# Two x loads on two queues ahead of the activation table load, and a landing reserve in the planner of a fused attention and GLU kernel

## The chip, the cores and the metric

The kernel runs on one core of one Trainium2 chip. The metric is the device time of one execution in microseconds; a smaller number is better. Executions of this kernel carry a span (first to last instruction) and the mean clock granted to TensorE; the time is the span plus about 2 us. Medians and lists of executions take in all of a run. The runs below were made on different chips; kernels ran with the kernel before beside them, and are compared with that.

Names used below: TensorE does matmuls (PE in the profile), VectorE is DVE, ScalarE is ACT, SyncE is SP. In the kernel before, all loads but two and all stores are issued by SyncE. A clock of 1.00 is full speed.

## The reference, cut to what matters

```python
xn = layernorm(x)                          # x: 1 x 2048 x 512, bf16
out = x + A(xn) + B(xn)
# A: linear attention, 32 heads of 16, feature map = softmax(+q W_phi), softmax(-q W_phi)
# B: h = (xn @ w_gate) * (xn @ w_up)       # 512 -> 1792
#    h @ w_down                            # 1792 -> 512
```

Everything waits for normalised tokens. There are 16 tiles of 128 tokens. Tiles 0 to 3 are loaded first, tiles 4 to 7 by one load of 512 KB, called x4 below.

## The kernel before: the parts that matter

Every instruction is a "step" with an estimated cost. A list scheduler in the Python file fixes the order of each engine from these estimates; the program gives each engine its instructions in that order, with waits on semaphores between engines. So an estimate that is wrong does no harm to the results, but it can put an instruction that must wait in front of one that need not. For loads:

```python
# in _plan(): when does a load land?
d0 = max(start + st.cost + 1500.0, dma_free)
dma_free = d0 + st.nbytes / 305.0          # ns, one queue of 305 GB/s
st.finish = dma_free
```

The issue order of the loads at the start:

```python
sc.step(ACT, ... preload_act_table_set("natural_log_exp_and_others"), name="tbl")
sc.step(ACT, ... activation(out=dum, in_=one1, func=Exp), name="dum")
load_x(SP, 0, 1)                # x0: tile 0, 128 KB
load_x(SP, 1, 1)                # x1: tile 1
load_gu(SP, "g", 0, 2)          # wg0: first gate slice
load_gu(ACT, "u", 0, 2)         # wu0: first up slice
# ... cut: further slices, in the order of the chain ...
sc.chain("x0 x1 wg0 x2 wg2 wu2 wg4 wu4 wT1 wv x4 wg8 wu8 x8 x12")
sc.chain("tbl dum wu0")
```

A unit U of the GLU takes two PSUM banks of a ring of six. ScalarE frees the gate bank, VectorE frees the up bank by the multiply:

```python
def U(ft, sg):
    bg, bu = nb(), nb()                                    # ring of six banks
    mm(group(bank(bg), ...wg...)); act_op(g, bank(bg))     # ScalarE frees bg
    mm(group(bank(bu), ...wu...))
    dve(... h = bank(bu) * g ..., name=f"h{ft}.{sg}")      # VectorE frees bu
```

The layer norm of a tile is, on VectorE, statistics (`bn_stats`, names st4, st5, ...), an aggregate (ag4), and, after two small ScalarE steps, the scaling. At the point that matters TensorE runs U(4), U(5), then a small product called FOLD, whose fourth part takes the bank that h4.0 (the multiply of U(4)) frees.

The softmax here doesn't subtract the row's maximum and nothing guards it: scores larger than these inputs give would overflow.

## Time and profile before

| quantity | value | view |
|---|---|---|
| median of the timed executions | 225.05 us (224.85 to 225.13) | times |
| time of the execution that was profiled | 227.54 us, span 225.5, clock 0.992 | times |
| TensorE busy | 218.3 us, 97% of the span | busy table |
| VectorE busy | 152.4 us, 68% | busy table |
| largest hole of TensorE | 1.96 us at 19.75 us | timeline |
| clock granted, 20 to 25 us | 0.69 on average | windows |

The timeline of TensorE of the kernel before. Columns: start in us, duration, engine, line, operation, output and input, shape, count, and in brackets the idle time before it and what ended it:

```profile
5.86 0.40 PE L448 MATMUL ps<-arena 128*128 128x128 bf16 x4 [0.73 <-DVE arena L576]
6.61 2.29 PE L448 MATMUL ps<-arena 128*128 128x128 bf16 x36 [0.35 <-DVE arena L576]
9.07 2.37 PE L448 MATMUL ps<-arena 128*128 128x256 bf16 x24 [0.17 <-DMA arena<-in_B_w_up_dram]
11.96 7.79 PE L448 MATMUL ps<-arena 128*128 128x256 bf16 x60 [0.53 <-ACT arena L420]
21.71 201.21 PE L448 MATMUL ps<-arena 128*128 128x128 bf16 x1174 [1.96 <-DVE arena L709]
```

The holes are in the brackets. The line at 11.96 is the narrow units and the first two wide ones, 7.79 us without a hole. Then TensorE waits 1.96 us for line 709, the multiply.

The timeline of VectorE of the same kernel shows why the multiply came late:

```profile
16.08 0.42 DVE L720 TENSOR_TENSOR arena<-ps,arena 128x256 bf16<-128x256 f32 x1 [0.45 <-ACT arena L420]
19.77 1.29 DVE L568 BATCH_NORM_STATS2 arena<-arena 128x6 f32<-128x512 bf16 x2 [3.27 <-DMA arena<-in_A_x_dram]
20.98 0.67 DVE L709 TENSOR_TENSOR arena<-ps,arena 128x512 bf16<-128x512 f32 x1
21.57 0.24 DVE L570 BATCH_NORM_AGGREGATE arena<-arena 128x2 f32<-128x6 f32 x2
```

VectorE was idle for 3.27 us until x4 landed, then did two statistics (1.29 us), and only then the multiply at 20.98, although U(4) was done at about 18.3 us (an estimate: in the changed kernel, below, the multiply starts as soon as TensorE has delivered, 6.30 us after the wide stage begins at 11.38; here that stage begins at 11.96). The chain of waits says the same; columns are start, duration and what it was:

```profile
12.34 7.41 DMA arena<-in_A_x_dram
...
20.39 0.68 DVE arena L568
21.06 0.60 DVE arena L709
...
21.71 200.79 PE ps L448 x1170
```

The windows view (stretch, its length, busy time and count of PE, weight loads, DVE, ACT, POOL, granted clock, DMA share, GB/s) shows what followed the hole:

```profile
20.00:25.00 5.00, 3.29 (x12) 1.37 (x13) 3.82 (x10) 3.13 (x9) 0.00 (x0) 0.69 0.82 268
25.00:30.00 5.00, 5.00 (x24) 2.25 (x23) 4.37 (x10) 2.25 (x5) 0.00 (x0) 0.97 0.28 58
```

For about 3.3 us TensorE ran at half clock (finer windows show 0.50 from about 21.95 to 25.3 us). Last, the end of the kernel, VectorE's last two instructions and SyncE's last two stores:

```profile
222.52 0.86 DVE L810 TENSOR_TENSOR arena<-ps,arena 128x256 bf16<-128x256 f32 x2 [2.56 <-PE ps L448]
222.97 0.81 SPq L172 DMA_DIRECT2D out_dram<-arena  x2
```

From VectorE's last instruction (222.52 + 0.86 = 223.38) to the end of the span (225.5) it is 2.12 us.

### The profile page before, as it was taken

The numbers are of one execution on the slowest core, as the hardware profiler recorded it, in microseconds if no ns is written. First come the engines' busy times: TensorE is split into PE (matmuls) and PEld (weight loads), VectorE is DVE, ScalarE is ACT, GpSimd is POOL, SyncE is SP. The second block draws the span as 40 slices with busy tenths as digits, with TensorE's granted clock in tenths as the row PEclk, the third lists the DMA queues.
The fourth block names the chain that finished last, engine by engine and source line by source line (L and its number), as shares of the span: only waits on it lengthen the run. The fifth ranks groups of instructions, "written<-read, shape, count | busy, mean of one in ns | idle before, by whom it ended". The sixth has DMA issues, their size and how long they took to land.

```text
span 225.5 us, 3354 instructions
## 1 busy us (share of the span) xinstructions
PE 218.3 (97%) x1308; PEld 108.3 (48%) x1308; DVE 152.4 (68%) x309; ACT 78.0 (35%) x160; POOL 38.7 (17%) x52
## 2 busy tenths in 40 slices
PE   7896999999999999999999999999999999999995
PEld 2763344444554454455444444444444444444454
DVE  3854699999958866779666548448447565745541
ACT  3642744543474334445212322222221321321100
POOL 5300011221131113122111101101101101101100
PEclk9999799999999999999999999999999999999999
DMA  6999347584300000002571334232132223124032
GB/s 178 312 270 374 92 101 127 120 274 117 49 0 0 3 0 0 1 3 47 116 79 40 93 93 26 70 93 70 26 93 70 54 67 93 30 63 96 29 88 71
DMA packets 48015, 19.89 MB, mean 88 GB/s; under 512 B 36848, under 2 KB 48000, under 8 KB 48000
## 3 DMA queue, kind: packets, MB, share of 16 engines
q1 hardware_dynamic: 47440, 19.41, 36.5%
q10 hardware_dynamic: 528, 0.26, 0.4%
q8 instruction: 10, 0.16, 0.3%
q14 instruction: 5, 0.04, 0.1%
q0 software_dynamic: 32, 0.02, 0.0%
HBM read 8.67 MB, written 2.10 MB: 48 GB/s over the span
## 4 chain that ended last, share of the span: by engine, by line
PE 89%; SPq 5%; DMA 3%; DVE 1%; issue 1%
PE ps L448 89%; DMA arena<-in_A_x_dram 3%; SPq L171 2%; SPq L172 2%; DVE arena L810 0%; DVE arena L568 0%; DVE arena L709 0%
## 5 line engine op out<-in xcount | busy, mean ns | idle before, releaser
L448 PE MATMUL ps<-arena 128*128 128x512 bf16 (+3 forms) x1298 | 214.1, 327 | 3.7 <-DVE arena L709 2.0
L448 PEld LDWEIGHTS ps<-arena 128*128 128x128 bf16 x1298 | 107.0, 98 | 111.3 <-DVE arena L709 2.4
L420 ACT ACTIVATE arena<-ps 128x512 bf16<-128x512 f32 (+2 forms) x138 | 72.6, 573 | 120.2 <-PE ps L448 120.0
L641 DVE TENSOR_REDUCE arena<-arena 128x64 f32<-128x1024 bf16 x32 | 38.8, 1213 | 39.3 <-ACT arena L420 39.3
L649 POOL TENSOR_TENSOR arena<-arena 128x512 bf16<-128x512 bf16 x32 | 33.8, 1055 | 171.2 <-DVE arena L647 171.2
L709 DVE TENSOR_TENSOR arena<-ps,arena 128x512 bf16<-128x512 f32 x52 | 35.4, 682 | 8.3 <-PE ps L448 7.6
L568 DVE BATCH_NORM_STATS2 arena<-arena 128x6 f32<-128x512 bf16 x16 | 10.4, 677 | 6.0 <-DMA arena<-in_A_x_dram 6.0
L793 DVE TENSOR_TENSOR arena<-ps,arena 128x512 bf16<-128x512 f32 x15 | 10.4, 690 | 4.1 <-PE ps L448 4.0
L768 DVE TENSOR_TENSOR arena<-ps,arena 128x512 bf16<-128x512 f32 x16 | 11.1, 691 | 0.6
L670 DVE TENSOR_TENSOR arena<-ps,arena 128x512 bf16<-128x512 f32 x16 | 10.2, 636 | 0.4 <-PE ps L448 0.4
L659 DVE RECIPROCAL arena<-arena 128x64 f32<-128x64 f32 x16 | 8.6, 538 | 0.0
L420 ACT ACTIVATE arena<-arena 128x2 f32<-128x2 f32 (+1 forms) x20 | 4.9, 252 | 10.3 <-DVE arena L570 9.9
L576 DVE TENSOR_SCALAR arena<-arena 128x512 bf16<-128x512 bf16 x16 | 6.1, 413 | 0.4 <-ACT arena L420 0.3
L647 DVE TENSOR_TENSOR arena<-arena 128x32 f32<-128x32 f32 x32 | 5.9, 184 | 0.4
L764 DVE RECIPROCAL arena<-arena 128x32 f32<-128x32 f32 x16 | 5.6, 352 | 0.5
L744 DVE RECIPROCAL arena<-arena 128x32 f32<-128x32 f32 x16 | 5.6, 351 | 0.4
L762 DVE SCALAR_TENSOR_TENSOR arena<-arena,ps 128x32 f32<-128x32 f32 x16 | 2.8, 172 | 4.2 <-PE ps L448 4.2
L819 PE MATMUL ps<-const-bfloat16-1.0 128*128 128x512 bf16 x10 | 4.3, 613 | 0.8 <-PEq L936 0.8
L673 DVE CAST arena<-arena 128x32 bf16<-128x32 f32 x16 | 4.6, 285 | 0.0
L720 DVE TENSOR_TENSOR arena<-ps,arena 128x256 bf16<-128x256 f32 x6 | 2.5, 421 | 2.3 <-ACT arena L420 2.3
L819 PEld LDWEIGHTS ps<-const-bfloat16-1.0 128*128 128x128 bf16 x10 | 1.3, 139 | 3.0 <-issue 3.0
L570 DVE BATCH_NORM_AGGREGATE arena<-arena 128x2 f32<-128x6 f32 x16 | 2.6, 166 | 0.2
(18 smaller groups left out, 11.3 us busy)
## 6 DMA issues: line engine op xcount, KB each, us to landing
out_dram<-arena SPq DMA_DIRECT2D x15, 128.0 KB, 2.0
arena<-in_B_w_down_dram SPq DMA_DIRECT2D x1, 1792.0 KB, 7.7
arena<-in_A_x_dram SPq DMA_DIRECT2D x3, 512.0 KB, 11.1
arena<-in_B_w_gate_dram SPq DMA_DIRECT2D x1, 768.0 KB, 9.0
arena<-in_B_w_up_dram SPq DMA_DIRECT2D x1, 768.0 KB, 10.5
arena<-arena SPq DMA_TRANSPOSE x44, 2.5
arena<-in_B_w_gate_dram SPq DMA_DIRECT2D x2, 256.0 KB, 5.1
arena<-in_B_w_gate_dram SPq DMA_DIRECT2D x1, 512.0 KB, 6.5
```

The source lines that it names most:

```text
L420: return e.activation(out=out_ap, in_=in_ap, func=func, scale=scale, **kw)
L448: ins = e.matmul(o, lhsT=l, rhs=r, start=s, stop=p, skip_group_check=True)
L568: dve(lambda e, t=t: e.bn_stats(stats_v[:, t, :], x_tile(t)), [x_tile(t)], [stats_v[:, t, :]], cost=560.0, name=f"st{t}", win=win)
L576: dve(lambda e, t=t: e.tensor_scalar(out=xn_tile(t), in0=x_tile(t), scalar1=mv_v[:, t, 0:1], scalar2=rstd_v[:, t:t + 1], op0=ALU.subtract, ...
L641: dve(lambda e: e.tensor_reduce(out=sm, in_=Et.rearrange("p (h f) -> p h f", f=16), axis=AX.X, op=ALU.add), [Et], [sm], cost=1130.0, name= ...
L647: dve(lambda e: e.tensor_tensor(out=ratio, in0=smv[:, :, 0], in1=rc, op=ALU.mult), [sm, rc], [ratio], cost=100.0, name=f"{name}q{t}")
L649: pool(lambda e: e.tensor_tensor(out=ev[:, :, 1, :], in0=ev[:, :, 1, :], in1=ratio[:, :, None].to_broadcast([128, H, 16]), op=ALU.mult), [ ...
L659: dve(lambda e: e.reciprocal(out=rs, in_=sm), [sm], [rs], cost=500.0, name=f"kc{t}")
L670: dve(lambda e: e.tensor_tensor(out=o1, in0=src, in1=rp_[:, :, :, None].to_broadcast([128, 8, 4, 16]), op=ALU.mult), [src, rs_v[:, t % 4, ...
L709: dve(lambda e: e.tensor_tensor(out=h, in0=bank(bu), in1=g, op=ALU.mult), [bank(bu), g], [h], name=f"h{ft}.{sg}")
L768: dve(lambda e: e.tensor_tensor(out=ov, in0=src, in1=wv4[:, :, :, None].to_broadcast([128, 8, 4, 16]), op=ALU.mult), [src, w], [o], cost=6 ...
L793: dve(lambda e: e.tensor_tensor(out=o, in0=bank(b), in1=x_tile(t), op=ALU.add), [bank(b), x_tile(t)], [o], name=f"fin{t}")
```

## The change

Its intent: x1 no longer queues behind x0 on SyncE, all later SyncE loads go out one slot sooner, and the planner stops believing in early landings, so that no engine has a waiting instruction ahead of one that is ready.

```diff
-                st.finish = dma_free
+                st.finish = dma_free + (2500.0 if st.nbytes > 300000 else 0.0)
...
-    alloc("dum", 32)
...
-    sc.step(ACT, lambda e: e.preload_act_table_set("natural_log_exp_and_others"), cost=1300.0, lat=0.0, name="tbl")
-    dum = sbv("dum", 0, 1)
-    one1 = nc.const_aps.tensor(1.0, [128, 1], BF16)
-    sc.step(ACT, lambda e: e.activation(out=dum, in_=one1, func=ACTF.Exp), writes=[dum], cost=120.0, name="dum")
     load_x(SP, 0, 1)
-    load_x(SP, 1, 1)
+    load_x(ACT, 1, 1)
     load_gu(SP, "g", 0, 2)
     load_gu(ACT, "u", 0, 2)
+    sc.step(ACT, lambda e: e.preload_act_table_set("natural_log_exp_and_others"), cost=1300.0, lat=0.0, name="tbl")
...
-    sc.chain("x0 x1 wg0 x2 wg2 wu2 wg4 wu4 wT1 wv x4 wg8 wu8 x8 x12")
-    sc.chain("tbl dum wu0")
+    sc.chain("x0 wg0 x2 wg2 wu2 wg4 wu4 wT1 wv x4 wg8 wu8 x8 x12")
+    sc.chain("x1 wu0 tbl")
```

The first line is the largest edit, since every order on TensorE, VectorE and ScalarE is planned anew from it.

## The prediction

> **What bounds it.** TensorE is the chain: 89% of the span in the chain of waits, busy 218.3 of 225.5 us (busy table). The timeline of TensorE shows 3.7 us of holes after the warm-up matmuls, all before 21.7 us: 0.73 (waits for the first normalised tile), 0.35 (the second), 0.17 (second up slice, a DMA), 0.53 (ScalarE copying a transpose), 1.96 at 19.75. After 21.71 us it runs 201 us without a recorded wait.
>
> **The large hole.** The wait list says TensorE waits 2.0 us for one VectorE multiply (gate times up, which frees a PSUM bank). That multiply was not short of data: the VectorE timeline is empty from 16.50 to 19.77, held by a DMA: the statistics of x tile 4, whose 512 KB load lands at 19.75. VectorE runs in order, two statistics (1.29 us) were planned ahead of the multiply, because the planner in the kernel thought x4 would land some 3 us sooner. TensorE then pays twice: the windows view grants clock 0.50 from about 21.96 to 25.3 us; weight loads of 512-wide matmuls are 0.427 us apart there, 0.213 elsewhere, so about 1.7 us is lost. The Trainium skill ("TensorE: Matmul & The Clock Gate", Part 1) describes this half clock after idleness; the trace agrees (427 ns against about 213). The hole's price is therefore 1.96 + 1.7 = 3.7 us.
>
> **What the change does.** (a) Loads over 300 KB count as landing 2.5 us later in the plan. All engine orders are planned from that, so the multiplies of the first wide units (bank releases) should go ahead of x4's statistics. Same work, other order. (b) x1 moves to ScalarE's queue, ahead of its first up slice; the table load (1.28 us) follows, and a dummy activation (0.20 us) goes. SyncE issues one load less at the start: 0.47 us sooner for all later ones. The table load should run about 1.8 to 3.1 us, before ScalarE's first work at 4.29, so it stays hidden.
>
> **How much is critical.** (a) nearly all of 3.7 us, if no hole of that size comes back. Give-back, estimated 0.3: x4's loads still land at about 19.4; a multiply that is ready then may sit behind a statistics instruction (0.68). VectorE is 90% or more busy from 28 to 62 us, and TensorE will be 3.7 us further ahead, with the six banks as its slack. (b) x1's statistics waited 0.34 us for the DMA; that goes. But the second up slice lands at 9.06 us and TensorE already waited 0.17 for it; the skill ("DMA: Bandwidth & Descriptors", Issuing engines are not separate DMA queues) says that queues share the 16 engines, and the windows show them saturated from 3 us (about 300 GB/s), so the bytes ahead of that slice stay and it lands at most slightly sooner. I estimate 0.15 us of gain.
>
> Sum: 225.05 - 3.7 + 0.3 - 0.15 = 221.5 us (1.6% faster). Range 220.2 to 223.9. Chances: faster by over 2% 0.2, within 2% 0.77, slower 0.03.
>
> **What would show it.** The 1.96 us hole gone from the TensorE timeline; clock 1.0 in the windows from 20 to 26 us; on VectorE the multiply of the first wide unit before the first statistics of x4; x1's statistics with no DMA wait; first real matmul at about 5.5 instead of 5.86; the wait for the second up slice longer than 0.17. No new wait on TensorE after 22 us above 0.5 us.
>
> **What would make it wrong.** A new stall past 1.5 us[...]: at 20 to 24 us for the large gate and up loads (landing 21.9 and 23.9), or at 30 to 60 us for VectorE. Then 223 to 225. If all startup holes shrink too, 220.

## The result, and the profile after

The changed kernel took 224.06 us (median; 224.03 to 224.61, 4 executions), the kernel before 225.09 us (224.85 to 225.50, 4 executions). The ratio is 0.9958, 95% interval 0.9937 to 0.9979: 0.4% faster. Ratios here and below are the mean time of one kernel's fast runs over that of the other's of the same rounds, so they are not quite the ratio of the medians quoted. The forecast of 221.5 us, range 220.2 to 223.9, was missed.

At first sight the profile contradicts the times. Its span fell from 225.5 to 222.0 us, by 3.5 us, just as predicted. The timeline of TensorE of the changed kernel:

```profile
5.47 0.40 PE L447 MATMUL ps<-arena 128*128 128x128 bf16 x4 [0.20 <-DVE arena L572]
6.18 4.68 PE L447 MATMUL ps<-arena 128*128 128x128 bf16 x60 [0.32 <-DVE arena L572]
11.38 207.18 PE L447 MATMUL ps<-arena 128*128 128x256 bf16 x1211 [0.53 <-ACT arena L419]
```

The hole at x4 is gone, the start is 0.58 us earlier at the third line, and no wait follows. VectorE of the changed kernel:

```profile
17.68 0.69 DVE L705 TENSOR_TENSOR arena<-ps,arena 128x512 bf16<-128x512 f32 x1 [1.75 <-PE ps L447]
18.29 0.68 DVE L564 BATCH_NORM_STATS2 arena<-arena 128x6 f32<-128x512 bf16 x1
18.89 0.68 DVE L705 TENSOR_TENSOR arena<-ps,arena 128x512 bf16<-128x512 f32 x1
```

The multiply (line 705 now) runs at 17.68, as soon as TensorE has delivered, ahead of the first statistic of x4. The clock in the windows view stays full:

```profile
20.00:25.00 5.00, 4.95 (x24) 2.24 (x23) 4.72 (x13) 3.93 (x11) 0.00 (x0) 1.00 0.95 268
```

And the end of the changed kernel:

```profile
218.17 0.86 DVE L806 TENSOR_TENSOR arena<-ps,arena 128x256 bf16<-128x256 f32 x2 [2.46 <-PE ps L447]
218.62 1.11 SPq L172 DMA_DIRECT2D out_dram<-arena  x2
```

From VectorE's last instruction (219.03) to the end (222.0) it is 2.97 us, 0.85 more than before. The two last stores take 1.11 us of SyncE instead of 0.81.

The contradiction is resolved by the times of the two profiled executions themselves. The one of before took 227.54 us, 2.5 us over its own median; the one of after took 224.04 us, its median. In both the time is the span plus 2.04 us. So the profile of before was not of an ordinary execution, and 2.5 of the 3.5 us are the difference between that execution and an ordinary one. That the spans differ by just what was forecast is luck: the 3.5 us are 0.58 of an earlier wide stage, 1.96 of the hole and 1.82 of a shorter run after it (201.21 - 199.39, where 199.39 is 207.18 less the 7.79 before the place of the hole), less 0.86 of a longer end.

### The profile page after: what moved, and what is told of

The parts are those of the page before. It is cut to its first block, busy times and chain, and to the rows that moved or that the text cites. A ratio compares the mean times of both kernels' runs of the same rounds, so it can differ in the third digit from the quotient of the medians.

```text
span 222.0 us, 3327 instructions
## 1 busy us (share of the span) xinstructions
PE 215.4 (97%) x1285; PEld 107.9 (49%) x1308; DVE 152.1 (69%) x309; ACT 78.0 (35%) x159; POOL 38.8 (17%) x52
## 4 chain that ended last, share of the span: by engine, by line
PE 94%; DVE 1%; DMA 1%; ACT 1%; issue 1%
PE ps L447 94%; DMA arena<-in_A_x_dram 1%; ACT arena L419 1%; DVE arena L564 1%; DVE arena L806 0%; DVE arena L566 0%; DVE arena L572 0%
## 5 line engine op out<-in xcount | busy, mean ns | idle before, releaser
L447 PE MATMUL ps<-arena 128*128 128x512 bf16 (+3 forms) x1275 | 211.0, 325 | 2.3 <-ACT arena L419 0.5
```

Source lines behind the costliest of these rows:

```text
L447: ins = e.matmul(o, lhsT=l, rhs=r, start=s, stop=p, skip_group_check=True)
```

## The experiments

Theory A: an ordinary execution of before has a smaller hole at x4 and no half clock, so there was only about 1 us to win. Rival theory B: the 3.7 us are lost in every execution of before, and the changed kernel gives 2.7 us back. After the first four runs two more theories were needed, for the end: C, it depends on what SyncE has gone through before; D, it belongs to something else in the changed kernel.

### The kernel before again

No edit; five rounds, for the span and clock of each execution.

> The kernel before, unchanged, run again for the span and clock of each execution. Theory A (the profiled execution of before, whose own time was 227.54 us against a median of 225.05, was an unusual one with a late x4 load): spans near 223.0 us, time minus span about 2.0 us as in both profiled executions, clock 0.998 to 1.000 in nearly all, and, if the profile is of an ordinary execution, a hole of 0.3 to 1.2 us instead of 1.96 and no half clock. Theory B (the hole of 3.7 us is in every execution and the changed kernel gives 2.7 us back elsewhere): spans near 225.5 us with clock 0.992, hole 1.9 us.

Measured: 225.07 us. The six spans are 222.9 to 223.8 us, the clock 0.999 or 1.000 in five of them and 0.992 in one. The profiled execution, again the slowest of its set (225.77 us), has this on TensorE:

```profile
11.75 7.79 PE L448 MATMUL ps<-arena 128*128 128x256 bf16 x59 [0.53 <-ACT arena L420]
21.23 200.00 PE L448 MATMUL ps<-arena 128*128 128x128 bf16 x1152 [1.69 <-DVE arena L709]
```

and this in the windows view:

```profile
20.00:25.00 5.00, 3.64 (x19) 1.48 (x20) 4.22 (x11) 3.47 (x10) 0.00 (x0) 1.00 0.84 274
```

The hole is there, 1.69 us, but no half clock follows it. Spans are those of theory A; the hole is longer than it expected, but in an execution that was 0.7 us over its median. If that excess is all in the hole, an ordinary one is about 1.0 us (an estimate from these two numbers; no profile of an execution at the median was taken). Theory B falls.

This profile also prices the half clock. TensorE's run after the hole is 200.00 us here and was 201.21 us in the first profile: 1.2 us more, not the 1.7 that the forecast took from the clock alone. The timeline of the weight loads (PEld, 20 to 30 us) shows where the rest may have gone. Just after the hole they wait twice at full clock:

```profile
22.55 0.55 PEld L448 LDWEIGHTS ps<-arena 128*128 128x128 bf16 x4 [0.55 <-DVE arena L709]
23.66 6.37 PEld L448 LDWEIGHTS ps<-arena 128*128 128x128 bf16 x31 [0.56 <-ACT arena L420]
```

In the first profile no pause just after the hole was longer than 0.28 us, and these came at every weight load; the slower matmuls took up time that is waited away otherwise.

### The changed kernel again

> The changed kernel again, same chip and rounds as the others. Both theories: 224.0 us, span 222.0, clock 1.000, no hole at x4.

Measured beside it: 224.18 us, 0.9963 of before (0.9950 to 0.9976), six spans from 222.0 to 222.6, clock 0.998 or more in all, no hole at x4:

```profile
11.73 207.30 PE L447 MATMUL ps<-arena 128*128 128x256 bf16 x1211 [0.53 <-ACT arena L419]
```

Set against the profile of before of the same chip, the difference of the spans (223.8 and 222.4) splits without a rest:

| part | before | changed | gain |
|---|---|---|---|
| wide stage of TensorE starts at | 11.75 | 11.73 | 0.02 |
| hole at x4 | 1.69 | 0 | 1.69 |
| TensorE from there to its last matmul | 200.00 | 199.51 (207.30 - 7.79) | 0.49 |
| TensorE's last matmul to the end | 2.57 | 3.37 | -0.80 |
| span | 223.8 | 222.4 | 1.40 |

7.79 us is the stretch of TensorE before the hole in the kernel before, which the changed kernel runs through in one piece of 207.30 us. The 0.49 us after the hole lie mostly in the two waits of the weight loads shown above: 0.55 and 0.56 us there, and in this profile (PEld, 19 to 30 us)

```profile
20.47 0.55 PEld L447 LDWEIGHTS ps<-arena 128*128 128x128 bf16 x4 [0.36 <-DVE arena L705]
21.23 8.85 PEld L447 LDWEIGHTS ps<-arena 128*128 128x128 bf16 x42 [0.21 <-ACT arena L419]
```

which is 0.54 us less.

### The reserve alone

```diff
-                st.finish = dma_free
+                st.finish = dma_free + (2500.0 if st.nbytes > 300000 else 0.0)
```

> The reserve of 2.5 us alone; x1 stays on SyncE's queue, table load and dummy first. TensorE's order is then that of the changed kernel, SyncE's that of before. Theory A: the ordinary hole goes, worth 0.3 to 1.2 us, so 224.0 to 224.8 us, and the hole at the first tiles stays (first real matmul at about 5.86 us). Theory B: about 221.7 us if the order is the cure of 3.7 us and something else in the change gives it back; 224.5 or more if the new order itself gives it back.

Measured: 224.43 us, ratio 0.9966 (0.9940 to 0.9993), within the noise of the whole change (0.9963). TensorE:

```profile
9.53 2.37 PE L448 MATMUL ps<-arena 128*128 128x256 bf16 x24 [0.51 <-DMA arena<-in_B_w_up_dram]
12.43 207.26 PE L448 MATMUL ps<-arena 128*128 128x256 bf16 x1211 [0.53 <-ACT arena L420]
```

No hole at x4; TensorE runs 207.26 us without a wait after 12.43, so the gain of about 0.5 us after the hole comes with the new order. The end is 2.05 us, the old length. The executions spread from 223.47 to 225.16 us; in the profiled one (224.22) TensorE waits 0.51 us at 9 us for the second up slice. That the spread comes from late first loads, which the hole had hidden, would fit, but is not shown; one execution (225.16) also had a clock of 0.992.

### The queue alone

```diff
-                st.finish = dma_free + (2500.0 if st.nbytes > 300000 else 0.0)
+                st.finish = dma_free
```

against the changed kernel, so x1 and wu0 stay on ScalarE's queue.

> x1 and the first up slice on ScalarE's queue ahead of the table load, dummy gone, no reserve. TensorE's order is that of before. On VectorE three statistics of x4 now stand ahead of the first wide multiply instead of two. Theory A: first real matmul at about 5.47 us, start gain 0.4 to 0.6 us, but TensorE reaches the multiply's wait that much sooner and x4's load does not land that much sooner, so the hole grows and the time stays within 0.3 us of before, or gets worse if the hole is long enough for the half clock (then up to 226 us). Theory B: 224.5 us, the start gain kept.

Measured: 226.23 us, ratio 1.0052 (1.0035 to 1.0068). This half of the change makes the kernel slower. TensorE and VectorE:

```profile
21.13 199.83 PE L447 MATMUL ps<-arena 128*128 128x128 bf16 x1152 [1.64 <-DVE arena L705]
```

```profile
18.53 1.29 DVE L564 BATCH_NORM_STATS2 arena<-arena 128x6 f32<-128x512 bf16 x2 [2.29 <-DMA arena<-in_A_x_dram]
...
19.82 0.66 DVE L564 BATCH_NORM_STATS2 arena<-arena 128x6 f32<-128x512 bf16 x1
20.40 0.67 DVE L705 TENSOR_TENSOR arena<-ps,arena 128x512 bf16<-128x512 f32 x1
```

x4 lands sooner (18.53 against 19.30 in the profile of before of the same chip), but the planner believed in it sooner still and put a third statistic ahead of the multiply, so the hole is 1.64 us. The end is 2.78 us, the long one. Start gain: none worth the name, the wide stage starts at 11.70 against 11.75. Against an ordinary execution of before, 0.67 us of longer end (2.78 - 2.11) and about 0.6 us of longer hole (1.64 less the estimate of 1.0) add up to 1.3 us; measured is 1.20 (226.23 - 225.03). The third statistic (0.66 us) more than took back what the sooner landing gave.

### Only the landing of x4, sooner and later

Two neighbouring loads are exchanged on SyncE after planning, so that TensorE, VectorE and ScalarE keep the order of before, the statistics ahead of the multiply included.

```diff
+    # later run: ("x4", "wg8") in place of ("wv", "x4")
+    for lst in (new_order[SP], global_order):
+        i, j = [next(k for k, st in enumerate(lst) if st.name == n) for n in ("wv", "x4")]
+        lst[i], lst[j] = lst[j], lst[i]
     sc.by_eng = new_order
```

> Kernel before with only two neighbouring loads of SyncE exchanged, x4 ahead of wv, after planning, so that all other engines keep the order of before, the two statistics ahead of the first wide multiply included. x4 should land about 1.6 us sooner (512 KB at about 330 GB/s). Theory A (in an ordinary execution of before the hole is only about 1.1 us and set by x4's landing): hole gone, clock 1.000, time about 224.1 us, 1.0 below before. If the order itself, or the half clock, cost 3.7 us in ordinary executions: 221.5 us.

Measured: 223.34 us against 225.33 (ratio 0.9922, 0.9874 to 0.9970; some of the executions of before beside it ran at the half clock). Without the executions under clock 0.995 the medians are 223.28 and 225.11, 1.8 us apart. TensorE has no hole from 11.58 us on:

```profile
11.58 207.73 PE L451 MATMUL ps<-arena 128*128 128x256 bf16 x1234 [0.53 <-ACT arena L423]
```

```profile
17.39 1.29 DVE L571 BATCH_NORM_STATS2 arena<-arena 128x6 f32<-128x512 bf16 x2 [1.26 <-DMA arena<-in_A_x_dram]
18.59 0.67 DVE L712 TENSOR_TENSOR arena<-ps,arena 128x512 bf16<-128x512 f32 x1
```

x4 lands at 17.39, and the two statistics are over before TensorE needs the bank. Repeated on another chip, beside the changed kernel:

> The exchange of x4 and wv alone in the kernel before, again, now on the same chip as the changed kernel: 223.3 us as the first time, 0.8 us under the changed kernel, with a single execution at the half clock (clock 0.992) about 1.6 us longer.

Measured: 224.13 us against 225.15, ratio 0.9956 (0.9934 to 0.9977). The first value was not reproduced: here the gain is 1.0 us (1.2 without the executions under clock 0.995), not 1.8, and this kernel isn't ahead of the changed one on the same chip (223.89, below). In its profile a hole of 0.16 us is left:

```profile
19.73 199.99 PE L451 MATMUL ps<-arena 128*128 128x128 bf16 x1174 [0.16 <-DVE arena L712]
```

Both runs together say that the ordinary hole is worth 1.0 to 1.8 us, and that the arrival of x4 alone, with the old order, sets it.

> Kernel before with x4 exchanged with the load after it (768 KB), all other engines in the order of before. x4 lands about 2.4 us later, so the hole is about 3.5 us instead of 1.1. If the half clock comes only with a hole long enough, it should now come in every execution: clock 0.99 or less, and the time rises by 2.4 plus about 1.7, to 229 us. If the half clock was a chance event of one profiled execution, the time rises by 2.4 alone, to 227.4, with clock 1.000.

Measured: 229.97 us, ratio 1.0197 (1.0129 to 1.0264, wide), with executions from 227.44 to 231.09, the last of them slow. The profiled one is the fastest:

```profile
22.77 200.00 PE L451 MATMUL ps<-arena 128*128 128x128 bf16 x1174 [3.49 <-DVE arena L712]
```

A hole of 3.49 us, as expected, and clock 1.000 in this execution: 227.44 us, the value expected without half clock. The other four have clocks of 0.992, 0.993, 0.985 and 0.985 and take 0.5 to 3.7 us longer. So a lowered clock came far more often here (4 of 5 executions), but not always. In the kernel before a clock under 0.995 was seen in 6 of the 38 executions of the experiments. Four of those six (224.96, 225.04, 225.16, 225.36 us) are no longer than their neighbours, two (227.28 and 228.10, the latter slow and left out of the ratios) are 2 to 3 us longer, as the first profiled one was. Where the half clock fell in unprofiled executions can't be told, since only their spans and mean clocks are known. The hole at x4 can't be behind all of it: 4 of the 51 executions of the repeated runs whose profile has no hole there, or one of 0.16 us, had such a clock too (225.16 in the reserve alone, 224.89 and 225.13 with x4 sooner, 225.42 with the load of 16 rows below).

### The end: does SyncE's past set it?

The length of the end was 2.05 to 2.13 us in all profiles with x1 on SyncE and 2.78 to 2.97 with x1 on ScalarE's queue. SyncE's instructions were counted in the built programs: 93 before the change and 92 after it (no view of the profile shows this count). First, a useless load was added in the quiet middle of the changed kernel, of 128 rows or of 16 (the lines that reserve the scratch area are cut here and below):

```diff
+    sc.dma(SP, scratch[0:128, :], x_flat[128:256, :], 131072, writes=[scratch[0:128, :]], name="pad")   # or 16 rows
-    sc.chain("x12 ... xT14 xT15")
+    sc.chain("x12 ... xT14 xT15 pad")
```

> The changed kernel with one useless load more on SyncE's queue, in the middle of the kernel (128 rows of 1 KB, the same as the load that had left that queue, into a scratch area nobody reads), so that SyncE again issues as many loads of as many rows as before. All engine orders else are those of the changed kernel. In the traces with x1 on ScalarE's queue the last store's issue starts 0.36 us after its data is ready (0.03 without), and the span ends 2.8 to 3.0 us after VectorE's last instruction instead of 2.1. Theory C (that end depends on what SyncE's queue or instruction stream has gone through before): the end goes back to 2.1 us, time 223.4 us against 224.2. Theory D (the end is something else of the changed kernel, or the queue of ScalarE being used): unchanged, 224.2 us.

> As the run with the 128-row useless load, but only 16 rows of 1 KB: one instruction more on SyncE, but an eighth of the rows. Theory C1 (the number of SyncE's instructions sets the end): 223.4 us, end 2.1 us, as with 128 rows. Theory C2 (the number of rows that went through SyncE's queue sets it): end stays at 2.8 to 3.0 us, 224.2 us, while 128 rows give 2.1. Theory D: both unchanged.

Measured: 223.76 us (end 2.06) and 223.70 us (end 2.07). The short end is back in both, so the number of rows doesn't matter. Theory D falls. Then a SyncE instruction that is no load:

```diff
+            # cut: by_name, a table of the steps by name
+                if st.name == "wo":
+                    for q in ("x0", "wg0"):                      # landed long ago
+                        e.wait_ge(dma_sems[by_name[q].lane[1]], 16)
```

> The changed kernel with one SyncE instruction more that is no DMA (waits for loads long complete, before the load of wo), 93 SyncE instructions as before the change instead of 92, but 32 plain DMA copies as in the changed kernel and no byte more. If the number of SyncE's instructions sets the length of the end: 2.1 us from VectorE's last instruction to the end, 223.5 us. If the number of DMAs issued on SyncE sets it: 2.8 to 3.0 us, 224.2 us.

Measured: 223.46 us, ratio 0.9927 (0.9907 to 0.9946), end 2.10 us:

```profile
218.94 0.86 DVE L810 TENSOR_TENSOR arena<-ps,arena 128x256 bf16<-128x256 f32 x2 [2.46 <-PE ps L451]
219.38 0.81 SPq L172 DMA_DIRECT2D out_dram<-arena  x2
```

The two last stores take 0.81 us again. The changed kernel on the same chip:

> The changed kernel again, same chip as the three others: 224.2 us, end 2.9 us.

Measured: 223.89 us, ratio 0.9943 (0.9924 to 0.9961), end 2.92 us:

```profile
218.12 0.86 DVE L806 TENSOR_TENSOR arena<-ps,arena 128x256 bf16<-128x256 f32 x2 [2.47 <-PE ps L447]
218.57 1.11 SPq L172 DMA_DIRECT2D out_dram<-arena  x2
```

One waiting instruction that does nothing shortens the end by 0.8 us in the profiles. In the times it is 0.43 us in the medians (223.89 to 223.46), which is not clear of the noise: the means of the six and six executions differ by 0.37 us, with a 95% interval from -0.1 to 0.9. The profile of the version with the wait also has 0.53 us of waiting for an up slice at its start, which that of the changed kernel has not.

Last, other counts of SyncE instructions, one look each (91: another load moved to ScalarE's queue, which spoils the start; 94, 96, 100: more idle waits).

> Changed kernel with the last load of x on ScalarE's queue as well: 91 SyncE instructions (its start may be slower, only the end is looked at). If any count below 93 is bad: end 2.8 to 3.0 us after VectorE's last instruction. If 92 alone is bad, or a period: 2.1 us.

> Changed kernel with two SyncE instructions more that only wait for loads long complete: 94. End 2.1 us in all cases except a period of 2 (then 2.9).

> Four SyncE instructions more: 96. End 2.1 us, or 2.8 to 3.0 if the bad count recurs every 4.

> Eight SyncE instructions more: 100. End 2.1 us, or 2.8 to 3.0 if the bad count recurs every 8 (or 4).

| SyncE instructions | end in us (one per profile) | last transfer of the queue q14, us from VectorE's last instruction |
|---|---|---|
| 91 | 2.11 | 1.4 after |
| 92 (changed kernel and queue alone) | 2.97, 2.91, 2.92, 2.78 | 0.9 to 1.2 after |
| 93 | 2.12, 2.11, 2.05, 2.13, 2.07, 2.11 (x1 on SyncE); 2.06, 2.07, 2.12, 2.10 (x1 on ScalarE's queue) | 1.0 to 1.2 before |
| 94 | 2.13 | 1.7 before |
| 96 | 2.09 | 6.5 before |
| 100 | 2.12 | 16 before |

Of the counts tried only 92 has the long end, in all four profiles; 91, 94, 96 and 100 have one profile each. They speak against a period of 1, 2, 4 or 8. That one SyncE instruction more brings the short end back is shown in four versions. The cause is not shown, but the traces hold a candidate, in the last column. The DMA view lists two queues of the kind "instruction", q8 and q14. The last transfer of q14, one packet of 0.01 MB, comes earlier the more instructions SyncE has. With 93 and more it lands before the last stores are issued, with 91 when their data have been moved. With 92 it falls between the last two stores, in all four profiles. The DMA view of the changed kernel (the repeat above, 219.5 to 220.5 us in 40 slices) shows it:

```profile
GB/s 287 328 328 369 185 184 124 62 21 0 0 0 0 0 0 0 0 0 0 0 0 328 0 0 0 0 0 82 123 184 266 287 287 328 328 206 184 103 62 21
q14 instruction: 1, 0.01, 3.9%
```

The first stretch is the next-to-last store, the single slice of 328 at 220.03 is q14, and the last store moves only after it. So SyncE probably waits for its own instructions at that point. No run moved this transfer without also changing the count, so it stays an inference.

### Both

The changed kernel with the useless 16-row load and with x4 ahead of wv:

> The changed kernel with the 16-row useless load (which gave the short end back) and with x4 ahead of wv on SyncE's queue; TensorE, VectorE and ScalarE keep the order of the changed kernel. In the changed kernel VectorE waits about 0.3 us for x4 after its first wide multiply, and TensorE does not feel it. So if the gains do not add (theory: both cures remove the same hole), it runs at 223.5 us like the padded kernel; if an earlier x4 still helps with the new order, 222.9 us or less.

Measured: 223.43 us, six executions from 223.19 to 223.64, ratio 0.9922 (0.9906 to 0.9937). It equals the kernel with the idle wait (223.46), so an earlier x4 adds nothing in the median where the order is already right. On the same chip both versions beat the kernel before (225.15). Against the changed kernel (223.89) this one is faster by 0.48 us in the means, 95% interval 0.2 to 0.8; for the idle wait alone the times don't show it, as said above.

## Why the prediction was wrong, point by point

**What failed: "The hole's price is therefore 1.96 + 1.7 = 3.7 us", with "(a) nearly all of 3.7 us" as the gain.** The mechanism was right: two statistics waiting for x4 stand ahead of the multiply, and the reserve puts it in front. The size was read from one execution that wasn't ordinary. In most executions (32 of 38) the half clock, 1.7 us of the 3.7, is absent, and even where it was profiled the run after the hole was only 1.2 us longer. The ordinary hole is about 1.0 us by the estimate above and worth 1.0 to 1.8 us by the exchange of loads. So the term of 3.7 us was really 1.0 to 1.8 us. The warning was at hand: the profiled execution took 227.54 us against a median of 225.05. Its own time should have been charged first: if that excess lies in the hole and the clock, 3.7 - 2.5 = 1.2 us is left for an ordinary execution.

The Trainium skill ("TensorE: Matmul & The Clock Gate", Part 1) says that the clock follows the activity in a window of 4096 cycles, 3413 ns, that runs freely and does not start with the kernel, so that clock changes vary from run to run. The prediction cited the page but used the half clock as a fixed price. The runs agree with the page so far as the one drop seen in a profile lasted about 3.3 us, and as the same program drops in some executions and not in others. The length of the hole alone didn't decide it: 1.69 us (no drop), 1.96 us (a drop), 3.49 us (no drop in the profiled execution, a lowered clock in four of five).

**What was not in the sum: the end.** The changed kernel's end is 0.8 us longer, in all profiles with 92 SyncE instructions. The prediction did not look at the end.

**Give-back of 0.3 us on VectorE, and its load from 28 to 62 us.** Wrong in sign. No new hole came in the changed kernel; with the new order TensorE's run after the place of the hole is 199.4 to 199.6 us instead of 199.8 to 200.0 (from the longest pieces of the timelines, those without half clock), a gain of about 0.5 us that was not predicted. It lies mostly in shorter waits of the weight loads just after the place of the hole (0.54 us between the two profiles above).

**Start gain of 0.15 us.** The details came true: x1's statistics no longer wait for the load, the first real matmul was at 5.47 us, the table load ran from 1.74 to 3.02 and stayed hidden. Its length of 1.28 us agrees with the Trainium skill ("ScalarE: Activation LUTs", What ACT_TABLE_LOAD costs), which gives 1283 ns. But over all profiles of comparable starts the wide stage begins at 11.83 us on average with x1 on SyncE (6 profiles, 11.50 to 12.43) and at 11.84 with it on ScalarE's queue (11 profiles, 11.34 to 12.52). The three profiles of the changed kernel itself lie at 11.34 to 11.73. No gain is clear of the scatter. The wait for the second up slice, predicted to grow beyond 0.17 us, was absent in all three profiles of the changed kernel; in six of its seven padded variants with the same first loads there was a wait for an up slice, of 0.17 to 1.06 us. The scatter of the first loads, up to 1.06 us of waiting for an up slice, is larger than the effect. This fits the Trainium skill ("DMA: Bandwidth & Descriptors", Issuing engines are not separate DMA queues): another issuing engine saves issue time, not transfer time.

**The sum with measured terms.** An ordinary hole of about 1.0, plus 0.5 after it, plus 0 at the start, less 0.8 at the end, is 0.7 us; measured 0.89 (225.07 to 224.18) beside it.

## What to carry to other kernels

Before a profile is priced, compare the profiled execution's own time with the median of the timed ones, and expect the excess in the largest events of it. In a list-scheduled kernel the order matters more than the queue: let an instruction that waits for a load never stand ahead of one that frees a buffer. Read the end of the kernel in every comparison of traces, since one SyncE instruction less moved it by 0.8 us here.

## What the Trainium skill lacked or had wrong

- "TensorE: Matmul & The Clock Gate", Part 1, gives an idle window of about 3.4 us for the half clock in its table of the two states. Here a hole of 1.96 us was followed by 3.3 us at half clock in one execution, and one of 3.49 us was not in another; how often a short hole is punished is not on the page (6 of 38 executions of the kernel before had a clock under 0.995, 4 of 5 with x4 later and a hole of 3.49 us in the profile, 4 of 51 with no such hole).
- No page says that the number of instructions on SyncE can lengthen the end of a kernel: 2.8 to 3.0 us with 92 instructions, 2.05 to 2.13 with 91, 93, 94, 96 or 100. "Runtime: NRT & Kernel Launch", Instruction fetch mechanics, speaks of blocks of 256 instructions; the last transfer of the instruction queue q14 falls between the last two stores with 92 instructions and at no other count tried, but no run here shows that it is the cause.
- No page that was used speaks of how much one and the same load scatters: in profiles of the kernel before VectorE's wait for x4 ended at 19.30 and at 19.77 us with the same issue order, and timed executions of it ranged from 224.6 to 227.3 us in the fast state, with one slow at 228.1.
